# Start of a fused attention and MLP kernel: first two token tiles through the V projection without 1/std, first V weights over ScalarE's queue

## The chip, the cores and the metric

The kernel runs on one core of a Trainium2 chip. The metric is the device time of one execution, in microseconds.

The profile names the engines as follows: PE is TensorE's matmuls, PEld its weight loads, DVE is VectorE, ACT is ScalarE, SP is SyncE. The DMA queues that SP and ACT issue to are SPq and ACTq; in the packet records they are q1 and q10.

## The reference, cut to what matters

```python
x = A_x                                                   # 1 x 2048 x 1024, bf16
x = x + _A_ref(_layernorm(x), A_wqkv, A_wo)               # attention over 8 dilated neighbours
x = x + _B_ref(_layernorm(x), B_w1, B_b1, B_w2, B_b2)     # MLP that mixes tokens
...                                                       # both once more
def _layernorm(x, axis=-1, eps=1e-5):
    m = jnp.mean(x, axis=axis, keepdims=True)
    v = jnp.var(x, axis=axis, keepdims=True)
    return (x - m) / jnp.sqrt(v + eps)
```

Only the very first step is touched: the layer norm of the input and V = norm(x) @ Wv. 1/std is one number for a row, so (x - mean) * rstd @ Wv is the same as ((x - mean) @ Wv) * rstd. This is what the change uses.

## The kernel before

Sixteen tiles of 128 tokens are loaded, normalised, transposed and multiplied by Wv in two groups of 512 columns (n = 0, 1). Each group (k, n) is 8 matmuls. The first five tiles are transposed by TensorE, the others by DMA. `start_up` holds a list of steps for each engine, and each engine takes its steps in exactly that order.

```python
def S_(k, cc): ...   # DVE: bn_stats of 512 columns        A_(k): DVE, bn_aggr -> mean, var
def R_(k): ...       # ACT: ln, exp -> 1/std
def N_(k, hs): ...   # DVE: x = (x - mean) * rstd, in place
def tr(k): ...       # PE: 8 transposes into PSUM
def C_(k, hf): ...   # ACT: copy 4 of them to hT
def V_(k, n, kts): ...                                    # PE: group (k, n) into an m tile
    # m_tile() comes from a pool of two PSUM buffers
def E_(k, n): ...    # ACT: copy the group to v, which frees its buffer
...
wm = m_tile()
for _ in range(14):                                       # warm-up matmuls on zeros
    chain_("PE", lambda: nc.tensor.matmul(wm[:], lhsT=warm[:, 0:P], rhs=warm[:], start=True, stop=True))
chain_("SP", x_load, 0, halves)
chain_("SP", x_load, 1)
chain_("SP", w_load, 0, 0)
chain_("SP", x_load, 2)
chain_("SP", w_load, 0, 1)
chain_("SP", x_load, 3)
chain_("SP", w_load, 1, 0)
chain_("SP", w_load, 1, 1)
...
pe = [(tr, 0), (V_, 0, 0, lo4), (tr, 1), (V_, 0, 0, hi4), (V_, 1, 0, lo4), (tr, 2), (V_, 1, 0, hi4),
      (V_, 2, 0, a8), (V_, 0, 1, a8), (tr, 3), (V_, 1, 1, a8), (V_, 2, 1, a8), (tr, 4)]
...
act = [(R_, 0), (C_, 0, 0), (R_, 1), (C_, 0, 1), (C_, 1, 0), (C_, 1, 1), (R_, 2), (E_, 0, 0), (C_, 2, 0), (C_, 2, 1),
       (E_, 1, 0), (R_, 3), (E_, 2, 0), ...]
dve = [(S_, 0, 0), (S_, 0, 1), (A_, 0), (S_, 1, 0), (N_, 0, halves), (S_, 1, 1), (A_, 1), (N_, 1, whole), ...]
```

The softmax here doesn't subtract the row's maximum and nothing guards it: scores larger than these inputs give would overflow.

## Time and profile before

| | before |
|---|---|
| time | 1297.89 us, median of 3 (1297.88 to 1298.09) |
| TensorE busy | 99% of a span of 1296.0 us |
| TensorE's share of the chain of waits | 97% |
| first transpose starts | 6.85 us |
| first matmul after the fifth transpose | 21.07 us; no gap from there on |

These lines are from the page of the kernel before. The first gives the span, the second busy time and share, the third the busy tenths in 40 slices, the last the chain that ended last.

```profile
span 1296.0 us, 19495 instructions
PE 1288.2 (99%) x8414; PEld 591.7 (46%) x8414; DVE 419.3 (32%) x851; ACT 373.4 (29%) x628; POOL 2.4 (0%) x15
...
PE   9999999999999999999999999999999999999998
...
PE 97%; DVE 1%; ACT 1%; issue 0%; DMA 0%; SPq 0%; DVEq 0%
```

TensorE is the bound nearly everywhere; only the start can give something. Next is the timeline of TensorE in the kernel before. The columns are start and length in us, engine, line, operation, output and input, number of instructions, and in brackets idle time and what ended it.

```profile
1.38 5.63 PE L268 MATMUL m<-warm 128*128 128x512 bf16 x14 [1.38 <-DVE warm L207]
6.85 0.61 PE L244 MATMUL s<-ident,x 128*128 128x128 bf16 x8
8.14 1.04 PE L255 MATMUL m<-wv,hT 128*128 128x512 bf16 x4 [0.68 <-ACT hT L249]
9.15 0.62 PE L244 MATMUL s<-ident,x 128*128 128x128 bf16 x8
...
20.62 0.61 PE L244 MATMUL s<-ident,x 128*128 128x128 bf16 x8
21.07 39.23 PE L255 MATMUL m<-wv,hT 128*128 128x512 bf16 x181
```

Line L268 is the warm-up, L244 a tile's eight transposes, L255 the V matmuls. Four V matmuls take 1.04 us: a new one starts every 0.216 us and the last one's end is counted too. The warm-up matmuls start 0.427 us apart until 6.05 us and 0.216 us apart from 6.42 us, so TensorE gets its full rate near 6.4 us, before real work begins.

The timeline of VectorE in the kernel before shows when x arrives:

```profile
3.22 1.29 DVE L226 BATCH_NORM_STATS2 bn<-x 128x6 f32<-128x512 bf16 x2 [1.90 <-DMA x<-in_A_x_dram]
4.54 0.21 DVE L230 BATCH_NORM_AGGREGATE mv<-bn 128x2 f32<-128x12 f32 x1
```

Tile 0: the second half landed at 3.78 us.

### The profile page before, as it was taken

How to read it: one execution, taken by the hardware profiler on the slowest of the kernel's cores; microseconds unless marked ns; L12 is line 12 of the kernel's file. 1: busy time of each engine (PE TensorE's matmuls, PEld its weight loads, DVE VectorE, ACT ScalarE, POOL GpSimd, SP SyncE). 2: the span in 40 equal slices, each digit the busy share in tenths (PEclk: the TensorE clock that was granted, in tenths of full speed). 3: DMA queues.
4: the chain of work that ended last, by engine and by line, in shares of the span. 5: the costliest groups of instructions: out<-in, count | busy, mean ns of one | idle time of the engine just before them, and what ended most of it. 6: DMA issues, size and time to landing. Idle time of an engine off the chain costs nothing.

```text
span 1296.0 us, 19495 instructions
## 1 busy us (share of the span) xinstructions
PE 1288.2 (99%) x8414; PEld 591.7 (46%) x8414; DVE 419.3 (32%) x851; ACT 373.4 (29%) x628; POOL 2.4 (0%) x15
## 2 busy tenths in 40 slices
PE   9999999999999999999999999999999999999998
PEld 4444444444444444444444444444444444444443
DVE  7457778810000022322300667688000000111111
ACT  5456665531111110000023666654211111000000
POOL 0000000000000000000000000000000000000000
PEclk9999999999999999999999999999999999999999
DMA  8411123652222235465510111246423222334330
GB/s 235 82 45 47 51 82 115 208 145 82 65 82 75 57 108 140 130 160 135 130 32 1 48 49 50 80 150 211 122 65 91 73 60 84 98 106 140 113 92 33
DMA packets 201574, 125.54 MB, mean 97 GB/s; under 512 B 39824, under 2 KB 183184, under 8 KB 201488
## 3 DMA queue, kind: packets, MB, share of 16 engines
q1 hardware_dynamic: 201488, 124.30, 33.8%
q8 instruction: 66, 1.08, 0.4%
q14 instruction: 20, 0.16, 0.0%
HBM read 96.48 MB, written 16.78 MB: 87 GB/s over the span
## 4 chain that ended last, share of the span: by engine, by line
PE 97%; DVE 1%; ACT 1%; issue 0%; DMA 0%; SPq 0%; DVEq 0%
PE m L352 17%; PE s L553 15%; PE s L510 15%; PE m L553 7%; PE m L510 7%; PE acc L510 7%; PE acc L553 7%; PE m L467 7%; PE m L337 4%; PE m L255 4%; PE s L383 2%; PE acc L418 1%; PE acc L422 1%; DVE xn L474 0%; PE m L268 0%; DVE Pm L398 0%
## 5 line engine op out<-in xcount | busy, mean ns | idle before, releaser
L510 PEld LDWEIGHTS <-w 128*128 128x128 bf16 x1792 | 175.4, 98 | 211.4
L553 PEld LDWEIGHTS <-w 128*128 128x128 bf16 x1792 | 175.3, 98 | 211.5
L352 PE MATMUL m<-hT,wqk 128*128 128x512 bf16 x1024 | 231.7, 380 | 0.0
L510 PE MATMUL s<-h,w 128*128 128x512 bf16 x896 | 202.8, 379 | 0.0
L553 PE MATMUL s<-g,w 128*128 128x512 bf16 x896 | 199.9, 379 | 0.0
L556 DVE SCALAR_TENSOR_TENSOR xo<-s,b_sb,xs 128x512 bf16<-128x512 f32 x32 | 24.0, 751 | 540.7 <-PE s L553 538.6
L352 PEld LDWEIGHTS <-wqk 128*128 128x128 bf16 x1024 | 95.3, 98 | 117.9 <-issue 10.7
L398 DVE TENSOR_TENSOR Pm<-pc,band 32x640 bf16<-32x640 bf16 x256 | 123.6, 483 | 65.8 <-ACT pc L386 56.3
L467 PE MATMUL m<-wo,oT 128*128 128x512 bf16 x512 | 112.5, 379 | 1.2 <-DVE xn L474 1.1
L510 PE MATMUL acc<-h,w 128*128 128x512 bf16 x448 | 103.9, 379 | 0.0
L553 PE MATMUL acc<-g,w 128*128 128x512 bf16 x448 | 100.6, 379 | 0.0
L553 PE MATMUL m<-g,w 128*128 128x512 bf16 x448 | 99.3, 379 | 0.0
L510 PE MATMUL m<-h,w 128*128 128x512 bf16 x448 | 99.0, 379 | 0.0
L174 ACT ACTIVATE ln<-mv,eps 128x1 f32<-128x1 f32 x64 | 18.9, 295 | 233.3 <-DVE mv L182 227.6
L517 ACT ACTIVATE g<-s,b_sb 128x1024 bf16<-128x1024 f32 x28 | 31.2, 1114 | 166.9 <-PE s L510 166.9
L467 PEld LDWEIGHTS <-oT 128*128 128x128 bf16 x512 | 49.5, 98 | 62.6 <-issue 4.5
L363 DVE COPY qB<-qs 32x512 bf16<-32x512 bf16 x136 | 38.1, 280 | 90.4 <-ACT qs L359 89.1
L255 PE MATMUL m<-wv,hT 128*128 128x512 bf16 x256 | 56.1, 379 | 0.7 <-ACT hT L249 0.7
L337 PE MATMUL m<-wv,hT 128*128 128x512 bf16 x256 | 55.4, 379 | 0.0
L359 ACT CAST qs<-m 128x512 bf16<-128x512 f32 x64 | 37.5, 586 | 49.0 <-PE m L352 49.0
L386 ACT ACTIVATE pc<-s,shift 128x640 bf16<-128x640 f32 x64 | 51.2, 799 | 0.3 <-PE s L383 0.3
L356 ACT CAST kT<-m 128x512 bf16<-128x512 f32 x64 | 37.5, 586 | 46.4 <-PE m L352 46.4
(57 smaller groups left out, 674.7 us busy)
## 6 DMA issues: line engine op xcount, KB each, us to landing
w<-in_B_w_dram SPq DMA_DIRECT2D x56, 512.0 KB, 3.8
w<-in_B_w_dram SPq DMA_DIRECT2D x64, 448.0 KB, 4.6
wqk<-in_A_wqkv_dram SPq DMA_DIRECT2D x16, 512.0 KB, 4.8
xa<-xn SPq DMA_DIRECT2D x32, 256.0 KB, 2.3
xs<-xa SPq DMA_DIRECT2D x32, 256.0 KB, 3.2
wv<-in_A_wqkv_dram SPq DMA_DIRECT2D x8, 512.0 KB, 5.5
wo<-in_A_wo_dram SPq DMA_DIRECT2D x8, 512.0 KB, 5.5
xr<-in_A_x_dram SPq DMA_DIRECT2D x16, 256.0 KB, 3.3
```

The source lines that it names most:

```text
L255: r = nc.tensor.matmul(pss_[k, n][:], lhsT=hT[:, kt, cols(*order[k])], rhs=wv[n][kt // 4][:, kt % 4, :], start=(kt == 0), stop=(kt == KD - 1))
L337: nc.tensor.matmul(ps[:], lhsT=hT[:, kt, cols(c, i)], rhs=wv[n][kt // 4][:, kt % 4, :], start=(kt == 0), stop=(kt == KD - 1))
L352: mm = nc.tensor.matmul(ps[:], lhsT=wts[part][:, kt, (g % 2) * P:(g % 2 + 1) * P], rhs=hT[:, kt, lo:lo + 512], start=(kt == 0), stop=(kt = ...
L356: nc.scalar.copy(out=kT[u % 2][:, ls], in_=ps[:])
L359: nc.scalar.copy(out=qs[:], in_=ps[:])
L363: nc.vector.tensor_copy(out=qB[u % 2][hp, h, ls], in_=qs[hp, :])
L386: nc.scalar.activation(out=pc[:].rearrange("p (n t) h k -> p n (t h k)", n=2), in_=ss[:, :, 0:2 * HG * GW], func=ACT.Exp, scale=scale, bia ...
L398: mm = nc.vector.tensor_tensor(out=Pm[rp, :, s0:s0 + HB, r * KG:r * KG + GW].rearrange("p h t k -> p t h k"), in0=pc[rp], in1=mk, op=ALU.mult)
L467: mm = nc.tensor.matmul(ps[:], lhsT=oT[g][:, cols(c, i)], rhs=wo[n][g // 4][:, g % 4, :], start=(g == 0), stop=(g == NG - 1))
L510: nc.tensor.matmul(pairs[fl][0][dc], lhsT=wt[c][:, i, fl * P:(fl + 1) * P], rhs=h2[c][i][:, dc * 512:(dc + 1) * 512], start=(k == 0), stop ...
L517: nc.scalar.activation(out=g[fb][:, fl, :].rearrange("p (n d) -> p n d", n=2), in_=t[:], func=ACT.Gelu_apprx_tanh, bias=b1_sb[:, ft:ft + 1])
L553: nc.tensor.matmul(aps[dc], lhsT=w2t[ft // HF][:, ft % HF, c::DIL], rhs=g[ft // GF][:, ft % GF, dc * 512:(dc + 1) * 512], start=(ft == 0), ...
```

## The change

The intent is to bring the first real matmul forward. The path from x to the first transpose loses ln, exp and the wait behind tile 1's statistics: tiles 0 and 1 are only centred (half of tile 0 by ScalarE), and 1/std becomes the scale of their evacuations. The first V weights are issued by ScalarE at once, and every later load of SyncE moves up by one place. Four warm-up matmuls go, since real work should start earlier. TensorE's and ScalarE's lists are ordered anew. The normalised tiles 0 and 1, which Q and K need, are made later and transposed by DMA.

```diff
-    ln_exp_table()
...
+        def B_(k): ...    # DVE: nm0 = -mean
+        def M_(k, h): ... # DVE: xc = x - mean
+        def Ma(k, h): ... # ACT: xc = x + nm0
...
         def E_(k, n):
-            return nc.scalar.copy(out=v[c][i][:, n * 512:(n + 1) * 512], in_=pss_[k, n][:])
+            dst, src = v[c][i][:, n * 512:(n + 1) * 512], pss_[k, n][:]
+            if k < 2:
+                return nc.scalar.activation(out=dst, in_=src, func=ACT.Identity, scale=rss[k])
+            return nc.scalar.copy(out=dst, in_=src)
...
-        for _ in range(14):
+        for _ in range(10):
...
+        chain_("ACT", w_load, 0, 0, nc.scalar)
+        chain_("ACT", ln_exp_table)
         chain_("SP", x_load, 0, halves)
         chain_("SP", x_load, 1)
-        chain_("SP", w_load, 0, 0)
+        chain_("SP", w_load, 0, 1)
         chain_("SP", x_load, 2)
-        chain_("SP", w_load, 0, 1)
+        chain_("SP", w_load, 1, 0)
         chain_("SP", x_load, 3)
-        chain_("SP", w_load, 1, 0)
         chain_("SP", w_load, 1, 1)
...
+        pe = [(tr, 0), (V_, 0, 0, lo4), (tr, 1), (V_, 0, 0, hi4), (V_, 1, 0, a8), (V_, 0, 1, lo4), (V_, 1, 1, lo4), (tr, 2),
+              (V_, 0, 1, hi4), (V_, 1, 1, hi4), (V_, 2, 0, a8), (tr, 3), (V_, 2, 1, a8), (tr, 4)]
+        act = [(Ma, 0, halves[1]), (C_, 0, 0), (C_, 0, 1), (R_, 0), (C_, 1, 0), (C_, 1, 1), (R_, 1), (R_, 2), (E_, 0, 0),
+               (E_, 1, 0), (C_, 2, 0), (C_, 2, 1), (R_, 3), (E_, 0, 1), (E_, 1, 1), (R_, 4), ...]
...
+            if k in (8, 9):
+                dve.append((N_, k - 8, whole))
...
+        sp = [(T_, k) for k in (*range(np_, NT), 0, 1)] + [(load_biases,)]
```

More of the change, by code (lines that the diff above doesn't have):

```diff
@@ L133 @@
                                 pattern=[[-1, GW]], channel_multiplier=1)
+    mv01 = const.tile([P, 2, 2], FP32, name="mv01")
+    rs01 = const.tile([P, 2], FP32, name="rs01")
+    nm0 = const.tile([P, 1], FP32, name="nm0")
     b1_bf = const.tile([P, FT], BF16, name="b1_bf")
@@ L187, in norm_dve @@
     def norm_dve(dst, x, mean, rs):
-        return nc.vector.tensor_scalar(out=dst, in0=x, scalar1=mean, scalar2=rs[:], op0=ALU.subtract, op1=ALU.mult)
+        return nc.vector.tensor_scalar(out=dst, in0=x, scalar1=mean, scalar2=rs, op0=ALU.subtract, op1=ALU.mult)
     def norm_act(dst, x, mean, rs):
@@ L205, in start_up @@
         np_ = 5
+        xc = [x2(f"xc{k}") for k in range(2)]
         warm = x2("warm", [P, 512])
@@ L217, in x_load, with w_load @@
             return r
-        def w_load(n, hf):
-            return nc.sync.dma_start(out=wv[n][hf][:], in_=wq_v[:, hf * (KD // 2):(hf + 1) * (KD // 2),
+        def w_load(n, hf, eng=nc.sync):
+            return eng.dma_start(out=wv[n][hf][:], in_=wq_v[:, hf * (KD // 2):(hf + 1) * (KD // 2),
                                                                 2 * D + n * 512:2 * D + (n + 1) * 512])
@@ L228, in A_, with B_, M_, Ma @@
         def A_(k):
-            mvs[k] = st("mv", [P, 2])
-            return nc.vector.bn_aggr(out=mvs[k][:], in_=sts[k][:])
+            mvs[k] = mv01[:, k, :] if k < 2 else st("mv", [P, 2])[:]
+            return nc.vector.bn_aggr(out=mvs[k], in_=sts[k][:])
+        def B_(k):
+            return nc.vector.tensor_scalar(out=nm0[:], in0=mvs[k][:, 0:1], scalar1=-1.0, scalar2=None, op0=ALU.mult)
+        def M_(k, h):
+            return nc.vector.tensor_scalar(out=xc[k][:, h], in0=xs[k][:, h], scalar1=mvs[k][:, 0:1], scalar2=None,
+                                           op0=ALU.subtract)
+        def Ma(k, h):
+            return nc.scalar.activation(out=xc[k][:, h], in_=xs[k][:, h], func=ACT.Identity, bias=nm0[:])
         def R_(k):
-            rss[k] = st("rs", [P, 1])
-            return rsqrt(rss[k][:], mvs[k][:, 1:2], 1.0, eps1)
+            rss[k] = rs01[:, k:k + 1] if k < 2 else st("rs", [P, 1])[:]
+            return rsqrt(rss[k], mvs[k][:, 1:2], 1.0, eps1)
         def N_(k, hs):
@@ L243, in tr @@
             for kt in range(KD):
-                r = nc.tensor.transpose(tps[k][:, kt, :], xs[k][:, kt * P:(kt + 1) * P], ident[:])
+                r = nc.tensor.transpose(tps[k][:, kt, :], (xc[k] if k < 2 else xs[k])[:, kt * P:(kt + 1) * P], ident[:])
             return r
@@ L284, in start_up @@
         a8 = range(KD)
-        pe = [(tr, 0), (V_, 0, 0, lo4), (tr, 1), (V_, 0, 0, hi4), (V_, 1, 0, lo4), (tr, 2), (V_, 1, 0, hi4),
-              (V_, 2, 0, a8), (V_, 0, 1, a8), (tr, 3), (V_, 1, 1, a8), (V_, 2, 1, a8), (tr, 4)]
+        pe = [(tr, 0), (V_, 0, 0, lo4), (tr, 1), (V_, 0, 0, hi4), (V_, 1, 0, a8), (V_, 0, 1, lo4), (V_, 1, 1, lo4), (tr, 2),
+              (V_, 0, 1, hi4), (V_, 1, 1, hi4), (V_, 2, 0, a8), (tr, 3), (V_, 2, 1, a8), (tr, 4)]
         pe += [(V_, k, n, a8) for k in range(3, NT) for n in range(NDC)]
-        act = [(R_, 0), (C_, 0, 0), (R_, 1), (C_, 0, 1), (C_, 1, 0), (C_, 1, 1), (R_, 2), (E_, 0, 0), (C_, 2, 0), (C_, 2, 1),
-               (E_, 1, 0), (R_, 3), (E_, 2, 0), (R_, 4), (E_, 0, 1), (C_, 3, 0), (C_, 3, 1), (R_, 5), (E_, 1, 1), (R_, 6),
-               (E_, 2, 1), (C_, 4, 0), (C_, 4, 1)]
+        act = [(Ma, 0, halves[1]), (C_, 0, 0), (C_, 0, 1), (R_, 0), (C_, 1, 0), (C_, 1, 1), (R_, 1), (R_, 2), (E_, 0, 0),
+               (E_, 1, 0), (C_, 2, 0), (C_, 2, 1), (R_, 3), (E_, 0, 1), (E_, 1, 1), (R_, 4), (C_, 3, 0), (C_, 3, 1), (E_, 2, 0),
+               (R_, 5), (C_, 4, 0), (C_, 4, 1), (E_, 2, 1), (R_, 6)]
         es = [(E_, k, n) for k in range(3, NT) for n in range(NDC)]
@@ L296, in start_up @@
                 act.append(rs.pop(0))
-        dve = [(S_, 0, 0), (S_, 0, 1), (A_, 0), (S_, 1, 0), (N_, 0, halves), (S_, 1, 1), (A_, 1), (N_, 1, whole),
+        dve = [(S_, 0, 0), (S_, 0, 1), (A_, 0), (B_, 0), (M_, 0, halves[0]), (S_, 1, 0), (S_, 1, 1), (A_, 1), (M_, 1, whole[0]),
                (S_, 2, 0), (S_, 2, 1), (A_, 2)]
@@ L305, in start_up @@
                 dve += [(S_, k + 1, 1), (A_, k + 1)]
+            if k in (8, 9):
+                dve.append((N_, k - 8, whole))
         dve.append((zero_fill,))
         dve.append((cast_biases,))
-        sp = [(T_, k) for k in range(np_, NT)] + [(load_biases,)]
+        sp = [(T_, k) for k in (*range(np_, NT), 0, 1)] + [(load_biases,)]
         qs = {"PE": pe, "ACT": act, "DVE": dve, "SP": sp}
-        need = {cast_biases: lambda: (load_biases,) in done, R_: lambda k: k in mvs, N_: lambda k, h: k in rss, tr: lambda k: (N_, k) in done, C_: lambda k, hf: k in tps,
-                V_: lambda k, n, kts: ((C_, k, 1 if kts[-1] == KD - 1 else 0) in done or (T_, k) in done), E_: lambda k, n: (V_, k, n) in done,
-                T_: lambda k: (N_, k) in done}
+        need = {cast_biases: lambda: (load_biases,) in done, R_: lambda k: k in mvs, N_: lambda k, h: k in rss, tr: lambda k: (N_, k) in done if k > 1 else (M_, k) in done and (k == 1 or (Ma, k) in done),
+                B_: lambda k: k in mvs, M_: lambda k, h: k in mvs, Ma: lambda k, h: (B_, k) in done, C_: lambda k, hf: k in tps,
+                V_: lambda k, n, kts: ((C_, k, 1 if kts[-1] == KD - 1 else 0) in done or (T_, k) in done), E_: lambda k, n: (V_, k, n) in done and k in rss,
+                T_: lambda k: (N_, k) in done and (k > 1 or (E_, k, 1) in done)}
         done = set()
@@ L322, in start_up @@
                     else:
-                        done.add((f, *(args if f is C_ else args[:1])))
+                        done.add((f, *(args if f in (C_, E_) else args[:1])))
     def load_wv():
@@ L560, in gemm2 @@
             mean, rs = stats(xo, 1.0, eps1)
-            norm_dve(xs[:], xo[:], mean, rs)
+            norm_dve(xs[:], xo[:], mean, rs[:])
             nc.sync.dma_start_transpose(out=hT[:, :, cols(c, i)], in_=xs[:])
```

## The prediction

> **What bounds the kernel.** The page gives TensorE 99% busy over 1296.0 us, and the chain of waits puts 97% of the span on it. In the timeline of TensorE the matmuls run without a gap from 21.07 us on, one 128x512 matmul each 0.216 us. So only the first 21 us are open to this change:
>
> - 14 warm-up matmuls from 1.38 us; twelve start 0.427 us apart, the last ones 0.216 us (the clock came up near 6.4 us).
> - Real work starts with the transpose of tile 0 at 6.85 us; its input was ready at 6.63 us.
> - Three idle stretches after that, by start times: 0.84 us (first copy of hT), 0.13 us, 0.61 us (normalising of tile 2).
> - The work before 21.07 us is 5 transposes of 0.447 us and 48 matmuls, 12.6 us; about 1.6 us are lost.
>
> **Removed.** Ln + exp (0.52 us) and bn_stats of tile 1, in front of the normalisation of tile 0 (0.6 us), leave tile 0's path to the transpose; ln + exp leave tile 1's. Four warm-up matmuls go (1.7 us).
>
> **Added.** One 128x1 multiply by -1 (0.21 us, as the bias product of the later normalisation), ScalarE centring 512 columns (an estimate of 0.7 us, from the 684 ns of the 128x512 activation with a bias), 0.1 us more for each of four evacuations with a scale, two extra normalisations (0.55 us) and two DMA transposes (1.23 us issue). The last two delay the first query/key weights from 54.3 us to about 58 us; they are needed at 65.96 us, so nothing is lost there.
>
> **Moved.** The first V weights (512 KB) are issued at 0.8 us instead of 2.19 us, beside x tile 0. [...] The trace has 0.18 to 0.25 MB/us before 3 us and 0.34 to 0.39 when full, so there is some room. I expect x0's second half at 4.2 us (3.78 before), x1 at 5.8 (5.27), x2 at about 8.5 (7.69), since it now comes behind two weight blocks.
>
> **Sum.** Tile 0's transpose starts near 6.1 us (6.85), tile 1's near 8.1 (9.15). But the first evacuation of PSUM now stands behind the rsqrt of tile 2 on ScalarE, and only two PSUM buffers serve these groups. So the third V group waits for x2's landing + 1.55 (stats) + 0.55 (rsqrt) + 0.7 (evacuation): an estimate of 11.3 us, with a TensorE gap of 0.3 us. A second gap of 0.7 us comes before tile 2's first group, whose buffer waits for copies, rsqrt and evacuation. I expect the fifth transpose to end at 20.4 us instead of 21.07: a gain of 0.7 us, all on the critical path.
>
> **Time.** 1297.2 us; 1296.2 to 1298.1 should hold it 8 times in 10. Within 2% is nearly certain: the whole open stretch is 1.6% of the time.
>
> **What would show it.** Landings of x0, x1, x2; start of the first transpose; TensorE idle time before 21 us, and who ends it (evacuation of v, not hT copies or normalisation); end of the fifth transpose; no wait for wqk at 65 us.
>
> **What would make it wrong.** If both queues fill the engines at once and x2 lands before 8 us, the gain may reach 1.5 us. If the shorter warm-up leaves the clock low for longer (idle gaps near 6 us), the first groups run at twice 0.216 us and the gain is gone. If x0 is delayed by a full 512 KB (1.4 us), tile 0 is no earlier.

The fifth transpose was to end at 20.4 us instead of 21.07 us, a gain of 0.7 us, so 1297.89 - 0.7 = 1297.2 us.

## The result, and the profile after

| | before | after |
|---|---|---|
| time, median of 6 | 1297.93 us (1297.06 to 1298.42) | 1299.60 us (1298.84 to 1301.11) |
| ratio, 95% interval | | 1.0015 (1.0003 to 1.0028) |
| second half of x tile 0 lands | 3.78 us | 5.67 us |
| x tile 1 / x tile 2 land | 5.27 / 7.69 us | 6.42 / 9.16 us |
| first transpose starts | 6.85 us | 7.13 us |
| TensorE at full rate | near 6.4 us | near 14.2 us |
| first matmul after the fifth transpose | 21.07 us | 24.34 us |

Ratios are the mean time of one kernel's fast runs over that of the other's of the same rounds, so not quite the ratio of the medians. The landings and the starts are from one trace each.

The change makes the kernel slower by 0.15%, some 2 us (1.7 us by the medians). The two profiled executions took 1297.71 and 1300.95 us; the 3.24 us between them are the 3.27 us in the last row of the table. So in this pair all of it comes from the first 24 us. The pair is not typical: the profiled execution of the change is the second slowest of its six. The page after:

```profile
span 1299.2 us, 19339 instructions
PE 1278.7 (98%) x8254; PEld 592.6 (46%) x8410; DVE 419.7 (32%) x853; ACT 373.9 (29%) x629; POOL 2.4 (0%) x15
...
PE   8999999999999999999999999999999999999998
...
PE 95%; DVE 1%; issue 1%; ACT 1%; DMA 1%; SPq 0%; DVEq 0%
```

Some 160 matmul records are missing in this trace, so its busy time is not compared with the one before. The timeline of TensorE after:

```profile
1.38 4.45 PE L284 MATMUL m<-warm 128*128 128x512 bf16 x10 [1.38 <-DVE warm L210]
7.13 1.10 PE L257 MATMUL s<-ident,xc 128*128 128x128 bf16 x8 [1.30 <-DVE xc L239]
8.91 1.89 PE L268 MATMUL m<-wv,hT 128*128 128x512 bf16 x4 [0.68 <-ACT hT L262]
10.59 1.06 PE L257 MATMUL s<-ident,xc 128*128 128x128 bf16 x8
11.45 5.72 PE L268 MATMUL m<-wv,hT 128*128 128x512 bf16 x19
...
17.66 1.89 PE L268 MATMUL m<-wv,hT 128*128 128x512 bf16 x8
19.99 1.89 PE L268 MATMUL m<-wv,hT 128*128 128x512 bf16 x8 [0.44 <-ACT v L276]
...
23.89 0.61 PE L257 MATMUL s<-ident,x 128*128 128x128 bf16 x8
24.34 1.89 PE L268 MATMUL m<-wv,hT 128*128 128x512 bf16 x7
```

Three things are to be seen. TensorE now stands idle before the first transpose, which starts later than before, not earlier. Four V matmuls at 8.91 us take 1.89 us, where before they took 1.04 us: TensorE runs at half rate (weight loads 0.43 us apart), and does so until 14.2 us. And a new wait of 0.44 us by the bracket, at 19.99 us, is ended by an evacuation of v.

The timeline of VectorE after shows why the first transpose is late:

```profile
3.56 0.69 DVE L229 BATCH_NORM_STATS2 bn<-x 128x6 f32<-128x512 bf16 x1 [2.24 <-DMA x<-in_A_x_dram]
...
5.69 0.69 DVE L229 BATCH_NORM_STATS2 bn<-x 128x6 f32<-128x512 bf16 x1 [1.43 <-DMA x<-in_A_x_dram]
...
6.66 0.15 DVE L236 TENSOR_SCALAR nm<-mv 128x1 f32<-128x1 f32 x1
```

VectorE waits 1.43 us for the second half of tile 0. What the DMA engines did meanwhile is in the DMA view of both kernels from 3.25 to 4.25 us, cut to the packets and the queues. First before, then after:

```profile
DMA packets 173, 0.27 MB, mean 271 GB/s; under 512 B 14, under 2 KB 67, under 8 KB 173
...
q1 hardware_dynamic: 173, 0.27, 80.6%
```

```profile
DMA packets 326, 0.33 MB, mean 334 GB/s; under 512 B 0, under 2 KB 326, under 8 KB 326
...
q10 hardware_dynamic: 326, 0.33, 96.9%
```

In this microsecond not one packet of SyncE's queue moved: all 326 belong to the V weights on ScalarE's queue. That load was issued from 0.80 to 1.27 us, the second half of tile 0 from 1.26 to 1.68 us. By the DMA views up to 3.25 and 4.25 us, SyncE's queue had moved 144 packets by the first time (the 128 of the first half, and 16 of under 512 B) and not one more by the second. It moved again from 4.29 us, beside the rest of the weights (last packet at 4.95 us), and the second half of tile 0 landed at 5.67 us.

### The profile page after: what moved, and what is told of

It is laid out like the page before. It is cut to its first block, busy times and chain, and to the rows that moved or that the text cites. A ratio compares the mean times of both kernels' runs of the same rounds, so it can differ in the third digit from the quotient of the medians.

```text
span 1299.2 us, 19339 instructions
## 1 busy us (share of the span) xinstructions
PE 1278.7 (98%) x8254; PEld 592.6 (46%) x8410; DVE 419.7 (32%) x853; ACT 373.9 (29%) x629; POOL 2.4 (0%) x15
## 4 chain that ended last, share of the span: by engine, by line
PE 95%; DVE 1%; issue 1%; ACT 1%; DMA 1%; SPq 0%; DVEq 0%
PE m L372 17%; PE s L573 15%; PE s L530 15%; PE acc L530 7%; PE m L530 7%; PE m L573 7%; PE acc L573 7%; PE m L487 7%; PE m L268 4%; PE m L357 4%; PE s L403 2%; PE acc L438 1%; PE acc L442 1%; DVE xn L494 0%; DVE Pm L418 0%
## 5 line engine op out<-in xcount | busy, mean ns | idle before, releaser
L372 PE MATMUL m<-hT,wqk 128*128 128x512 bf16 x963 | 223.3, 379 | 6.2 <-issue 4.6
```

The source lines that it names most:

```text
L372: mm = nc.tensor.matmul(ps[:], lhsT=wts[part][:, kt, (g % 2) * P:(g % 2 + 1) * P], rhs=hT[:, kt, lo:lo + 512], start=(kt == 0), stop=(kt = ...
```

## The experiments

Theories: **Queue** (the weights on ScalarE's queue get ahead of x), **Clock** (with fewer warm-up matmuls and an idle time after them, TensorE stays at half rate for longer) and, as a rival of both, **Order** (evacuations wait behind rsqrts on ScalarE). All kernels gave correct results. Each call had its own rounds of the kernel before, on its own chip, so ratios are compared, and times only within a call.

| run | what | time, us (range of 5) | ratio to before |
|---|---|---|---|
| e1_warm14 | change, 14 warm-ups | 1299.27 (1298.74 to 1299.63) | 1.0008 |
| e2_spq | change, SyncE's queue only | 1297.42 (1296.94 to 1297.86) | 0.9995 |
| e3_spq_warm14 | both | 1297.62 (1296.91 to 1298.11) | 0.9996 |
| e4_before_warm10 | before, 10 warm-ups | 1297.92 (1297.00 to 1299.20) | 0.9999 |
| f1_before_actq | before, weights on ScalarE's queue | 1299.09 (1298.10 to 1299.51) | 1.0008 |
| f2_table_first | change, table load first | 1300.25 (1299.32 to 1300.80) | 1.0017 |
| f3_spq_order | e2 with evacuations earlier | 1296.19 (1296.08 to 1296.70) | 0.9988 |
| f4_best | f3, loads and idle matmuls | 1296.21 (1295.98 to 1297.11) | 0.9989 |
| g1_late_issue | change, weights issued at 2.43 us | 1301.77 (1300.84 to 1302.17) | 1.0031 |
| g2_warm6 | f3 with 6 warm-ups | 1298.09 (1297.24 to 1298.23) | 1.0003 |
| g3_pieces | change, weights in four loads | 1299.26 (1298.12 to 1300.85) | 1.0015 |
| g4_x0_two_queues | f4, half of x on ScalarE's queue | 1296.33 (1295.93 to 1296.69) | 0.9992 |

The 95% interval of each ratio is about 0.0013 to either side, so single ratios near 1 decide nothing; pairs with separate ranges of times do. The kernels before of the three calls ran 1297.35 to 1298.87, 1297.20 to 1298.59 and 1296.43 to 1298.87 us.

### e1_warm14: the change with 14 warm-up matmuls

```diff
-        for _ in range(10):
+        for _ in range(14):
```

> The changed kernel with 14 warm-up matmuls instead of 10, nothing else. Three theories of the 1.7 us (3.2 us in the profiled pair) that the change costs. Clock: ten warm-up matmuls end at 5.6 us, TensorE then stands idle until 7.1 us and again at 8.0 us, and the full rate (0.216 us between matmuls instead of 0.427) comes at 14.2 us instead of 6.4 us. This theory expects the full rate before 10.9 us here, the fifth transpose's end below 22.5 us (24.3 in the change, 21.07 before), and a time of 1297.0 to 1298.3. Queue: what costs is x tile 0's second half, which lands at 5.67 us instead of 3.78 us behind the V weights; untouched here, so a time of 1299.0 or more. Order: what costs is the evacuations behind the rsqrts on ScalarE; untouched, 1299.0 or more.

The time was 1299.27 us, where Clock had asked for at most 1298.3. In the trace, the timeline of TensorE:

```profile
1.38 4.86 PE L284 MATMUL m<-warm 128*128 128x512 bf16 x14 [1.38 <-DVE warm L210]
7.13 0.89 PE L257 MATMUL s<-ident,xc 128*128 128x128 bf16 x8 [0.90 <-DVE xc L239]
8.70 1.04 PE L268 MATMUL m<-wv,hT 128*128 128x512 bf16 x4 [0.68 <-ACT hT L262]
...
21.61 4.56 PE L268 MATMUL m<-wv,hT 128*128 128x512 bf16 x20
```

The full rate was there at 4.8 us, and the matmul after the fifth transpose came at 21.61 us, as Clock expected. But the first transpose still started at 7.13 us, all five times lie above Clock's range, and the median is 1.1 us above that of the kernel before in the same call (ratio 1.0008; its interval, 0.9996 to 1.0021, still holds 1). So Clock alone is refuted. Clock can explain the difference between the ratios 1.0015 and 1.0008, about 0.9 us, but the ranges of the two kernels overlap.

### e2_spq: the V weights back on SyncE's queue, 10 warm-up matmuls

```diff
-        chain_("ACT", w_load, 0, 0, nc.scalar)
...
         chain_("SP", x_load, 1)
-        chain_("SP", w_load, 0, 1)
+        chain_("SP", w_load, 0, 0)
         chain_("SP", x_load, 2)
-        chain_("SP", w_load, 1, 0)
+        chain_("SP", w_load, 0, 1)
         chain_("SP", x_load, 3)
+        chain_("SP", w_load, 1, 0)
         chain_("SP", w_load, 1, 1)
```

> The changed kernel with the first V weights back on SyncE's queue in their old place, still 10 warm-up matmuls. Queue: x tile 0's second half lands at 3.8 us again, the first transpose starts near 5.7 us, and the time is 1296.5 to 1297.5. Clock: the first transpose starts near 5.7 us too, [...] so in most runs the full rate comes late (after 9.5 us) and the time is 1298.3 to 1300, with a spread between runs of over 1 us. Order: near 1299.

The time was 1297.42 us, in Queue's range and below Clock's. The second half of tile 0 landed at 3.71 us and the first transpose started at 5.62 us, 0.42 us behind the start of the last warm-up matmul. So here the ten of them reached up to real work without a hole. The gap before the first V matmul was there (0.68 us), and the four behind it ran at full rate (1.04 us) all the same:

```profile
1.38 4.45 PE L284 MATMUL m<-warm 128*128 128x512 bf16 x10 [1.38 <-DVE warm L210]
5.62 0.79 PE L257 MATMUL s<-ident,xc 128*128 128x128 bf16 x8
7.09 1.04 PE L268 MATMUL m<-wv,hT 128*128 128x512 bf16 x4 [0.68 <-ACT hT L262]
```

All five times lie below all six of the change, though in another call. The cut of the warm-up fits an x that comes early; with the late x it leaves a hole.

### e3_spq_warm14: SyncE's queue and 14 warm-up matmuls

The edit is both of the two above.

> The changed kernel with the first V weights back on SyncE's queue and 14 warm-up matmuls: only the centring is left of the change. Clock: full rate near 6.4 us as before; the first transpose waits for the warm-up matmuls until 6.9 us, tile 1 is earlier than before, time 1296.5 to 1297.9, so equal to the kernel before or up to 1.4 us below it. Order: the evacuations behind the rsqrts keep it at 1298.5 or more. Queue: same as Clock here, so the pair with the run before it is what counts.

It measured 1297.62 us, as Clock and Queue expected and against Order. The full rate came near 7.0 us and the first transpose started at 7.17 us, behind the warm-up. Against e1, with the same warm-up, only the queue differs: the ranges are separate, and the ratios 1.0008 and 0.9996 differ by 0.0012, about 1.6 us. The two traces do not show this cost: their first matmuls after the fifth transpose are only 0.24 us apart (21.61 and 21.37 us), because the full rate came at 4.8 us in e1 and at 7.0 us in e3, where the warm-up itself held up the first transpose. These are one of the faster executions of e1 and the slowest of e3. Against e2 the 4 warm-up matmuls made no difference (0.9996 and 0.9995).

### e4_before_warm10: the kernel before with 10 warm-up matmuls

```diff
-        for _ in range(14):
+        for _ in range(10):
```

> The kernel before with 10 warm-up matmuls instead of 14, nothing else. Clock: TensorE stands idle from 5.65 to about 6.65 us and again near 7.4 us, so in most runs the full rate comes after 9.5 us; time 1298.8 to 1301. Queue and Order: no part of their cause is in it, 1297.5 to 1298.3.

Clock expected at least 1298.8 us; the median was 1297.92 us. The range is 2.2 us wide, so this run decides nothing about the time. Its trace shows what the clock did in one execution. It changed at 4.48, 7.89 and 11.30 us, 3.41 us apart, and these are windows of that length (start and end, length, busy us of the engines with the number of instructions, then the granted TensorE clock, DMA share and GB/s):

```profile
1.07:4.48 3.41, 3.10 (x8) 1.15 (x9) 1.54 (x3) 1.01 (x1) 1.94 (x9) 1.00 0.57 170
4.48:7.89 3.41, 1.68 (x13) 0.68 (x12) 2.35 (x6) 1.32 (x5) 0.00 (x0) 1.00 1.03 345
7.89:11.30 3.41, 3.41 (x15) 1.76 (x14) 2.56 (x5) 1.65 (x5) 0.00 (x0) 0.50 1.03 346
11.30:14.70 3.40, 3.40 (x23) 1.67 (x22) 2.05 (x4) 2.61 (x8) 0.00 (x0) 1.00 1.06 382
```

The full rate came at 4.48 us. In the window after that TensorE was busy for only 1.68 us, and then the granted clock was halved (0.50) for one window of 3.41 us. (The 1.00 of the first window is no reading: no record of the clock exists before its first change. There the spacing of the matmuls has to be read, 0.427 us.)

No threshold of TensorE's busy time comes out of these traces. Over stretches of the same length, the full rate was kept after 1.72 us busy of 3.42 us (f1, 4.36 to 7.78 us) but lost after 1.74 us of 3.41 us (g3, 4.07 to 7.48 us). It came after 2.69 us (g3, 0.66 to 4.07 us) but not after 2.74 us (the change, 7.40 to 10.82 us, counted back from the full rate at 14.2 us). Some of these stretches hold transposes; whether these count like other matmuls was not tested.

### f1_before_actq: the kernel before with only the queue changed

```diff
+        chain_("ACT", w_load, 0, 0, nc.scalar)
+        chain_("ACT", ln_exp_table)
         chain_("SP", x_load, 0, halves)
         chain_("SP", x_load, 1)
-        chain_("SP", w_load, 0, 0)
+        chain_("SP", w_load, 0, 1)
...
```

> The kernel before, with only the first V weights moved to the head of ScalarE's queue (normalisation and 14 warm-up matmuls as before). Queue: the weights get ahead of x tile 0's second half on the DMA engines; that half lands near 5.7 us instead of 3.8 us, the first transpose starts near 7.5 us instead of 6.85 us, and the time is 0.8 to 1.8 us above the kernel before. Clock (the warm-up matmuls are untouched): within 0.4 us of the kernel before.

The time was 1299.09 us, ratio 1.0008, so about 1.0 us. The second half of tile 0 landed at 5.71 us and the first transpose started at 7.73 us, both within 0.3 us of what Queue expected. The traces agree: the first matmul after the fifth transpose starts at 22.05 us, 0.98 us later than in the kernel before. The move of this load makes the kernel slower by the medians (1299.09 and 1297.85 us). The interval of the ratio still holds 1, and the ranges overlap from 1298.10 to 1298.59 us, but four of five times lie above the whole range of before or within 0.06 us of its top. The edit also moves SyncE's later loads up by one place, so that x tile 2 comes behind a second block of weights. In f4 below it does so too, landing at 9.04 us, and f4 is as fast as f3; so that alone is not the harm.

### f2_table_first: ScalarE's first two instructions swapped

```diff
-        chain_("ACT", w_load, 0, 0, nc.scalar)
         chain_("ACT", ln_exp_table)
+        chain_("ACT", w_load, 0, 0, nc.scalar)
```

> The changed kernel with the two first instructions of ScalarE swapped: the activation table is loaded first (1.28 us), the first V weights are issued after it, so near 2.1 us, still on ScalarE's queue, still 10 warm-up matmuls. If the harm is that the weights get ahead of x tile 0, that half lands at 3.8 to 4.2 us, the first transpose starts before 6.2 us and the time is 0.8 us or more below the change, near 1297.5. If a second queue is harmful by itself, whenever it is used, the time stays within 0.5 us of the change, near 1299.5.

This missed its purpose. The timeline of ScalarE shows it:

```profile
0.80 1.28 ACT L113 ACT_TABLE_LOAD   x1 [0.80 <-PEq L691]
0.83 0.46 ACTq L223 DMA_DIRECT2D wv<-in_A_wqkv_dram  x1
```

The load was issued at 0.83 us, while the table load was still running, and the second half of tile 0 landed at 5.70 us as in the change. So it is the change once more, by accident useful: 1300.25 us, ratio 1.0017, with the full rate at 13.7 us in its trace. It repeats the result, and its range and that of f3 are 2.6 us apart.

### f3_spq_order: evacuations before rsqrts

```diff
-(R_, 1), (R_, 2), (E_, 0, 0),
+(R_, 1), (E_, 0, 0), (R_, 2),
...
-(C_, 2, 1), (R_, 3), (E_, 0, 1), (E_, 1, 1),
+(C_, 2, 1), (E_, 0, 1), (R_, 3), (E_, 1, 1),
```

The base is e2.

> The run with all loads on SyncE's queue and 10 warm-up matmuls, with two places exchanged in ScalarE's list: the evacuation of group (0,0) before the rsqrt of tile 2, that of group (0,1) before the rsqrt of tile 3. Order: the gap of 0.60 us on TensorE before tile 2's first group goes, and the time is 0.3 to 0.7 us below the run without the exchange (1297.42), so 1296.7 to 1297.1. Queue and Clock: nothing of their causes changes, the same time within 0.3 us.

The time was 1296.19 us, 0.5 us below the expected range. The wait before tile 2's first group fell from 0.60 to 0.19 us between issue times: the view now prints 16 V matmuls as one piece behind the third transpose, where in e2 there were 8, a gap and 8.

```profile
13.52 0.61 PE L257 MATMUL s<-ident,x 128*128 128x128 bf16 x8
13.97 3.80 PE L268 MATMUL m<-wv,hT 128*128 128x512 bf16 x16
17.61 0.61 PE L257 MATMUL s<-ident,x 128*128 128x128 bf16 x8
```

So Order is not what makes the change slow (e2 has the same order and is not slow), but it holds back a part of its gain: 0.41 us of gap by the traces, and 0.0007 by the ratios, about 0.9 us. This kernel's whole range lies below that of the kernel before in the same rounds (ratio 0.9988, interval 0.9976 to 1.0001).

### f4_best: a candidate with two more edits

```diff
-        chain_("SP", x_load, 2)
         chain_("SP", w_load, 0, 1)
+        chain_("SP", x_load, 2)
...
-        pe = [(tr, 0), (V_, 0, 0, lo4), ...
+        pe = [(tr, 0), (F_, 2), (V_, 0, 0, lo4), ...        # F_: matmuls on the warm-up tile
```

> The candidate for a version better than both: the run before it, with the second half of the V weights for the first group loaded before x tile 2 (the first group waited 0.58 us for it), and two idle matmuls on the warm-up tile after the first transpose, so that TensorE is not idle until the clock is up. 0.3 to 1.2 us below the run before it, 1295.8 to 1296.8; no gap above 0.25 us on TensorE between the first transpose and 24 us except the one before the first V group (below 0.6 us of idle).

It measured 1296.21 us, no better than f3, although the fifth transpose starts 0.52 us earlier in its trace (19.26 us, 19.78 in f3) and the largest gap left is 0.42 us. So the gaps were as expected and the time was not. The time from there to the end differs between traces by more than this: in the traces, the stretch from the first matmul behind the fifth transpose to the end is 1274.2 to 1275.6 us, with the same program in it. Half a microsecond at the start can't be told from that in five runs.

### g1_late_issue: the V weights on ScalarE's queue, but later

```diff
         nc.vector.memset(warm[:], 0.0)
+        nc.vector.memset(wv[0][0][:].rearrange("p k n -> p (k n)"), 0.0)
```

> The changed kernel, where VectorE first clears the tile of the first V weights (about 1.1 us, until about 2.4 us, while it has nothing else to do), so that their load on ScalarE's queue can't be issued before that; still 10 warm-up matmuls. The run that put the table load first did not delay the issue (0.83 us in its trace), so this is the test that it should have been. If the harm is that the weights get ahead of x tile 0's second half, it lands below 4.2 us (5.67 in the change), the first transpose starts below 6.2 us (7.13), and the time is 1.2 us or more below the change: 1296.9 to 1298.2. If use of the second queue is harmful whenever it comes, the second half stays above 5 us and the time above 1299.

The first half of the expectation held: with the issue at 2.43 us the second half of tile 0 landed at 3.87 us and the first transpose started at 5.62 us. So the use of a second queue did not harm x here (3.87 us, 3.78 before); the issue ahead of x did (5.67 us). But the time was 1301.77 us, the slowest of all, because now the weights lost: SyncE had issued the other half of them at 2.20 us, that load got ahead, and the first half landed at 10.43 us. The timeline of TensorE:

```profile
5.62 1.06 PE L258 MATMUL s<-ident,xc 128*128 128x128 bf16 x8
10.47 0.85 PE L269 MATMUL m<-wv,hT 128*128 128x512 bf16 x2 [3.79 <-DMA wv<-in_A_wqkv_dram]
```

### g2_warm6: the clock without the queue

```diff
-        for _ in range(10):
+        for _ in range(6):
```

The base is f3.

> The run with all loads on SyncE's queue and the exchanged order on ScalarE (1296.19), with 6 warm-up matmuls instead of 10: they end near 4.1 us and TensorE stands idle for about 1.3 us until the first transpose at 5.4 us, about as long as in the change (1.48 us), while x lands as early as before. Clock: the full rate comes after 9 us in most runs, and the time is 0.7 us or more above 1296.19 with a larger spread than its 0.6 us. If only the queue matters: within 0.3 us of 1296.2.

The time was 1298.09 us, ratio 1.0003 against 0.9988, so about 1.9 us above f3, which ran in another call. No time lies in f3's range. x landed nearly as early as in f3 (3.79 and 3.62 us), and the trace has the full rate at 10.3 us:

```profile
1.38 2.74 PE L284 MATMUL m<-warm 128*128 128x512 bf16 x6 [1.38 <-DVE warm L210]
5.26 1.10 PE L257 MATMUL s<-ident,xc 128*128 128x128 bf16 x8 [1.14 <-DVE xc L239]
7.04 1.89 PE L268 MATMUL m<-wv,hT 128*128 128x512 bf16 x4 [0.68 <-ACT hT L262]
```

This is the change's picture again: a hole behind the warm-up, then four matmuls in 1.89 us. By the ratios a hole of this kind costs about 1.9 us by itself; in the two traces the first matmul after the fifth transpose is 0.79 us apart (21.02 and 20.23 us), so the size is uncertain. 1.9 us is more than the whole gain of 0.7 us that the change was after. Nor does every hole cost as much: f1's trace has one of 1.70 us and kept the full rate.

### g3_pieces: the V weights in four loads

```diff
-        chain_("ACT", w_load, 0, 0, nc.scalar)
+        for kt in range(4):
+            chain_("ACT", lambda: nc.scalar.dma_start(out=wv[0][0][:, kt], in_=wq_v[:, kt, 2 * D:2 * D + 512]))
```

> The changed kernel with the first V weights in four loads of 128 KB instead of one of 512 KB, all at the head of ScalarE's queue; 10 warm-up matmuls. If the two queues are served load by load in order of issue, x tile 0's second half comes behind one or two pieces and lands at 3.9 to 4.8 us, the first transpose starts at 5.8 to 6.6 us, time 1297.3 to 1298.8. If ScalarE's queue simply goes first while it has work, it lands at 5.4 us or later and the time is near 1299.5.

The statistics of tile 0's second half began at 4.97 us: earlier than in the change (5.69 us), later than expected. The first transpose started at 6.41 us, as expected. The time, 1299.26 us, missed the range from above. In its trace the full rate came at 4.07 us, was lost at 7.48 us and came back at 14.31 us, so the clock has a share in it. The DMA engines together moved less from 3.75 us on. In windows, with GB/s as the last column:

```profile
2.50:3.75 1.25, 1.25 (x4) 0.46 (x3) 0.06 (x1) 1.08 (x1) 0.85 (x4) 1.00 1.05 331
3.75:6.00 2.25, 1.27 (x5) 0.35 (x3) 1.59 (x4) 0.20 (x1) 0.00 (x0) 1.00 0.62 166
```

x tile 1 landed at 8.19 us (6.42 us in the change), so tile 1 was late instead of tile 0. Why the rate fell to 166 GB/s was not tested.

### g4_x0_two_queues: half of x tile 0 on ScalarE's queue

```diff
-                r = nc.sync.dma_start(out=xs[k][:, h], in_=xin_v[c, i][:, h])      # both halves
+                ...                                                               # second half: nc.scalar.dma_start
...
-        for _ in range(10):
+        for _ in range(9):
```

The base is f4.

> The candidate (1296.21) with the second half of x tile 0 on ScalarE's queue, so that both halves are issued at 0.8 us, and 9 warm-up matmuls. ScalarE's queue then carries nothing else early. The second half lands near 3.3 us (3.67), the first transpose starts near 5.3 us (5.62), x1 lands 0.3 us earlier; 0 to 0.6 us below the candidate: 1295.6 to 1296.2.

The second half landed at 3.73 us (3.67 in f4) and the first half at 3.56 us (3.15 in f4), so nothing was won for tile 0 and the first transpose started at 5.62 us as in f4. The time, 1296.33 us, is that of f4 within the noise. The expectation was wrong: issued together, both halves landed later than one after the other on one queue.

## Why the prediction was wrong

**The bound and the stretch were right.** Only the first 21 us (now 24) changed; what follows took 1274.9 us in both profiled executions, and no wait for the query/key weights appeared: they landed at 59.5 us (58 expected).

**The step that failed first is the DMA step.** "I expect x0's second half at 4.2 us (3.78 before)". It landed at 5.67 us. The author took the two queues to share the engines, so that x would lose a little (0.4 us); no trace had shown that. The trace shows x standing still while all 326 packets from 3.25 to 4.25 us are the weights'. The third condition that I named as making it wrong ("If x0 is delayed by a full 512 KB (1.4 us)") is what happened, with 1.9 us. With it "tile 0's transpose starts near 6.1 us" became 7.13 us, although the shortened path held: from the statistics' start at 5.69 us it takes 1.44 us. e2, g1 and f1 show this cause from both sides: x back to 3.7 or 3.9 us when the weights don't go first, x at 5.7 us when they do. Its cost with equal warm-up is about 1.6 us (e1 against e3).

**The second step that failed follows from the first.** The sum took the clock for granted, and named the risk only at the end: "If the shorter warm-up leaves the clock low for longer". Ten warm-up matmuls end near 5.6 us. That suits a first transpose at 5.6 us, not one at 7.13 us. In the profiled run the full rate came at 14.2 us instead of 6.4 us. g2 against f3 puts such a hole at about 1.9 us by the ratios with no change of the queue (0.79 us by the traces), and e2 against e3 shows that ten warm-up matmuls cost nothing without a hole. How much it costs in the mean of the change's runs is less sure: the ratios of the change and e1 (1.0015, 1.0008) give 0.9 us, with overlapping ranges.

**The sum of the terms.** Centring alone gives -0.5 us (e3, 0.9996, not clear of noise by itself), the queue adds 1.6 us (e1 against e3), the cut warm-up 0.9 us (the change against e1): together +2.0 us, by construction the measured 0.0015. The prediction had -0.7 us for all. The split is uncertain, since each ratio has about 1.7 us to either side. In the traced executions it is the other way round: of the 3.27 us at the first matmul after the fifth transpose, 2.73 us lie between the change and e1 (warm-up and clock) and 0.54 us between e1 and the kernel before. Each of these is a single execution in which the full rate came at its own time. So it is shown that the queue makes x late and costs time (f1, and e1 against e3), and not how the loss is divided.

**What was right.** The gap of 0.7 us before tile 2's first group, by the evacuation behind rsqrt and copies, measured 0.60 us between issue times in the traces of the change, e1, e2 and e3, and an exchange in ScalarE's list cut it to 0.19 us (f3). The smaller gap of 0.3 us at the third group did not appear, because at half rate TensorE came there late itself (about 15.4 us instead of 11.3 us); in e1 and e3 it was 0.16 us. The evacuations with a scale took 0.67 us against 0.59 us, 0.1 us more as predicted. Centring by ScalarE took 0.72 us (0.7 predicted), the negated mean 0.15 us (0.21).

**What stays open.** Why the DMA engines moved nothing but the weights from 3.25 to 4.25 us, rather than alternating, is not shown; the traces show only the order of packets. With a load of 128 KB on ScalarE's queue instead of 512 KB they did mix: in g4, 157 packets of q1 and 123 of q10 moved from 2 to 3 us. Nor do single traces tell how often the late clock strikes.

## What to carry to other kernels

Before moving a load to another queue, ask which load the first compute step waits for, and check in the trace where that one lands. Here 512 KB of weights, issued on a second queue 0.46 us ahead of x's second half, made it land at 5.67 us instead of 3.78 us; issued at 2.43 us, behind it (g1), they left it at 3.87 us. When warm-up matmuls are shortened because work comes earlier, check in the trace that it does: a hole of over a microsecond behind them went with a full rate only at 10.3 us in g2 and at 14.2 us in the change, though f1 kept the full rate over a hole of 1.70 us. A change whose parts were made to fit each other (early data, short warm-up, new order of the evacuations) should be measured part by part; here the parts that were kept, with the old queue and two exchanged evacuations (f3, ratio 0.9988), ran below the kernel before in the same call.
